# Transformer layer with segment memory, one core: another order of the first transposes and projections, nine more filler products, two-part masks without a wait between their parts, and a new order list

## The chip, the cores and the metric

The kernel runs on one NeuronCore of a Trainium2 chip. The metric is the time of one execution on the device, in microseconds (us). Engines: PE is TensorE (its weight loads are shown apart as PEld), DVE is VectorE, ACT is ScalarE, POOL is GpSimd, SP is SyncE, which here issues all DMA transfers.

## The reference

A pre-norm layer over 2048 tokens of width 640, in bf16: attention with 32 heads of 20, in four segments of 512 tokens, each with a causal softmax inside the segment and a linear memory of the segments before it; then an MLP of inner width 1728 with SiLU.

```python
phi = lambda t: jnp.where(t > 0, t + 1.0, jnp.exp(t))
for s in range(N):                                   # N = 4 segments of L = 512
    logits = jnp.einsum('bhqd,bhkd->bhqk', qs, ks) * scale + mask
    a_dot = jnp.einsum('bhqk,bhkd->bhqd', _softmax(logits, axis=-1), vs)
    num = jnp.einsum('bhld,bhde->bhle', phi(qs), M)
    den = jnp.einsum('bhld,bhd->bhl', phi(qs), z)[..., None] + 1e-06
    outs.append(g * (num / den) + (1.0 - g) * a_dot)
    M = M + jnp.einsum('bhld,bhle->bhde', phi(ks), vs)
    z = z + jnp.einsum('bhld->bhd', phi(ks))
...
h = x + _A_ref(_layernorm(x, axis=-1), A_wq, A_wk, A_wv, A_wo, A_beta)
h2 = h + _B_ref(_layernorm(h, axis=-1), B_w1, B_w2)  # silu(y @ w1) @ w2
```

## The kernel before

The four segments follow one another, overlapped: while the attention of one segment runs, the projections of the next and the MLP of the one before are put between. A segment is 4 blocks of 128 tokens.

Every step is a named task. In the order list a task stands as `name/engine:slots`; the suffix A, D or G puts a step on ACT, DVE or POOL, C runs a product as four 32-column products side by side, W makes one exponential of 2048 columns out of two of 1024, and the numbers are buffer slots (of PSUM banks, where PE is concerned). The list is the whole order: each engine runs its tasks in the order in which they stand there, and waits on semaphores for what it needs from others. A recorder (`Tracker`) works out these waits from what each instruction reads and writes.

The names that matter here, for block i of segment 0 and group g of 4 heads:

- `x0`, `x1`, `x2`: loads of block 0, block 1, and blocks 2 and 3 together. `w_q0`, `w_q1`, `w_k0`, `w_k1`: the query and key weights in two pieces each. `x4`, `x8`: later blocks.
- `fill`: products of zeros that nobody reads, at the start (L625).
- `n1_st`, `n1_rs`, `n1_ap`: statistics (DVE, for block 2 ACT), reciprocal root (POOL) and normalising (DVE) of a block; `n1_mn2` is the mean of block 2 on ACT. `n1_tp` transposes the block with five products against the identity (L816), and `n1_te` brings the result from PSUM into `tT` (ACT L825 or DVE L826).
- `pr000x`, `pr000y`, `pr001x`, `pr001y`: the first query and key projection, in halves of two token blocks (x is blocks 0 and 1, y is blocks 2 and 3), straight from the loaded weights as 32-column products (L740). Those that follow (`pr010` and on, L553 and L554) read weights that `re_` tasks have copied into another order (L733 and L735). `qe` brings a projection out of PSUM; `lsc0` is a small ACT step on the gate.
- `qk`, `e`, `mk`, `av`: scores (L991), exponential (ACT, L1012, or L1008 in one piece), causal mask (POOL, L1024) and weighted sum (L1047). The first exponential is `e0a2`. Score tiles a have one masked square, tiles b and e have two.
- `ex`, `pa`, `pb`: the three parts of phi. `kt` transposes phi of the keys by DMA into `phiKt` for the memory products; `vpad2` and `ve00` prepare the values of segment 0.
- `h1`, `th`, `s`, `h2`, `o`, `out`: the MLP and the output.

Where a task is several instructions of one engine, `run` records them: the first and the last carry the task's reads, the last its writes. For a task that reads and writes the same tile, such as a mask of two squares, the last instruction thus finds a read by the first and waits on POOL's own semaphore for it.

Of the kernel before, what the change touches and what calls it, by code (L numbers as in the profile page):

```python
# [6 lines left out]
ALU = mybir.AluOpType  # L7
# [37 lines left out]
class Tracker:  # L45
# [288 lines left out]
D = 640  # L334
# [36 lines left out]
x0:0 zpad:0 iota fill25:7 vpad0 x1:3 halfc mq0 x2:5,6 warm:0 w_q0:0 w_q1 n1_st0:5 w_k0:0 w_k1 w_wv:0 sel n1_st1:3  # L371
n1_rs0 epsc beta n1_ap0:1 fill5:5 n1_rs1 n1_st2:0,3 n1_st3:1 n1_tp0:0 n1_ap1:0 n1_mn2 n1_rs2 n1_te0:0 n1_rs3 n1_tp1:0
n1_ap2 re_wq1/G:0 n1_te1 n1_tp2:3 n1_ap3:2 x4:4,1,2,7 n1_te2/D x8:8,9,11,10 n1_tp3:6 re_wk0/G pr000x.0:2 n1_te3 re_wq3
pr000x.1 re_wq4/G pr001x.0:1 re_wk2/A qe000x/D:0 pr001y.0:5 re_wk1 pr000y.0:0 re_wq2/G re_wk3/A pr001y.1 pr001x.1
pr000y.1 qe001y qe001x/D eps0 pr010.0/C:2 qe000y re_wk4/G pa001:0 lsc0 ex001:0 qk0a0:4,0 pr010.1 vpad2 e0a2:3
pr011.0:7 re_wq0/G qe010/D:0 e0a0 pr011.1 lsc1 qk0b0:0,2 qe011/D pr020.0:6 e0b2:6 n1_st5:1 pr021.0:7 e0b0 qk0e0:4,2
n1_st6:2 pr020.1 e0e2:5 v00.0:0 pb001 n1_rs6 qe020/D:0 e0e0 v00.1 kt00:0 n1_st4:4 pr021.1 ve00:0 qk1a0:2,4 qe021/D
v02.0:6 e1a0:4 n1_rs4 v01.0:0 n1_st10:3 vt09:0 e1a2 n1_rs5 v01.1 vt06 pa011:1 mk0a ex021:2 qk1b0:4,2 ve01/D zf0 v02.1
mk1a e1b2:1 n1_ap4:2 mk0b v03.0:0 lsc2 ve02/D e1b0 n1_tr4:1 v03.1 lsc3 pa021:2 ex011:1 mk0e qk2a0:6,2 n1_ap5:0
pr040.0:4 e2a0:2 w_w1_1:0 ve03/D pr031.0:5 n1_tr5 e2a2 mq1 zf1 n1_st7:6 pr031.1 pr030.0:7 qe031:0 vt03 n1_st8:5  # L380
qk2b0:0,2 n1_rs7 ex031:0 pr030.1 vt00 e2b0:0 pr041.0:5 mq2 n1_ap6:1 qe030/D pr041.1 n1_rs8 n1_tr6 e2b2 pr040.1 pb011
qe041/D:0 mk1b av0:6 qe040 pa041:0 ex041:1 qk2e0:2,0 oe0/D:1 vt04 e2e0:3 n1_rs10 av1:5 n1_ap7:0 vt01 mk2b oe1/D:0
v10.0:4 e2e2 vt08 n1_st11:7 qk3a0:2,6 vt05 v10.1/C e3a2:1 mq3 mk2a vt07 ve10/D:0 e3a0 qk3b0:0,6 vt010 n1_st9:4
v11.0/C:4 e3b0:6 mk3a v11.1 mqr mk2e e3b2 vt02 qk4a0:0,2 ve11/D vt011 e4a2:4 td1:6 mk3b av2:7 nm1:1,1 n1_tr7 e4a0
oe2/D:0 qk4b0:3,5 vpad1 av3:2 e4b0:2 n1_ap10:3 n1_rs11 td2:7 e4b2 oe3/D:0 nm2:1 qk4e0:3,0 pr120.0:2 mk4b e4e0:5 pb041
pr120.1/C n1_ap8:2 e4e2 kt04:2 qk5a0:3,6 n1_rs9 pb021 pr100.0:5 qe120/D:0 e5a0:1 mm1 w_wo:0 pr100.1/C mk4e e5a2 w_w1_4
qe100/D:0 qk5b0:3,1 td3/C:0 n1_tr10:0 nm3:1 e5b2/W:3 v12.0:6 mzz mk4a n1_ap11:0 v12.1 kt01:1 mk5a pa100:0 td0/C:0 ve12
pa120:0 qk6a0:1,3 mk5b nm0:1 pr110.0/C:5 w_w1_3 e6a0:6 pa031:0 kt02:4 pr110.1 e6a2 qk6e0:1,6 qe110/D:0 av5:0 e6e2:0
pr111.0:5 e6e0 n1_tr8 pr111.1/C qk6b0:6,3 qe111/D av4:2 mk6e e6b0:3 n1_tr11 oe5/D:0 pr101.0/C:5 e6b2 pa110:0 qk7a0:0,6
oe4/D:1 w_w1_0 pr101.1 e7a2:1 mk6b n1_ap9:1 td4:2 pr130.0:3 e7a0 qe101/D n1_tr9 pr130.1 mk6a nm4:3 qk7b0:4,6 mk7a  # L390
e7b0:2 pb031 td5/C:2 v13.0/C:0 qe130/D:0 e7b2 kt03:3 v13.1/C nm5:2 av6:4 ex120:1 mk7b pa130:0 ex110:0 qk8a0:2,5 ve13/D
pr131.0:7 e8a0:4 mm0 pr131.1 oe6/D:0 e8a2 av7:0 qe131/D qk8b0:3,1 oe7/D:1 td6/C:7 e8b2:5 pr141.0:5 nm6:3 td7/C:0 e8b0
qk8e0:1,6 nm7:2 pr141.1/C e8e2:3 mk8b pr140.0:3 ot0:0 qe141/D:0 e8e0 pr140.1 pa101:0 qk9a0:6,4 mk8a qe140/D ot1 mz00:0
e9a0:6 mz02 mz03 mk8e pr121.0/C:1 pb110 mz04 e9a2 ot2 qk9b0:2,6 eps1 mz01 pr121.1/C e9b0:0 ma0:0 wo0.0:4 qe121/D e9b2
pb120 qk10a0:0,2 vt17:0 wo0.1 e10a0:2 mk9b vt19 wo1.0:6 rs0 e10a2 vt16 wo1.1 mk9a ot3 ex100:0 qk10b0:4,0 rs1 wo2.0:2
# [985 lines left out]
```

## Time and profile before

| | |
|---|---|
| median of 3 runs | 295.2 us (294.46 to 297.48) |
| the profiled execution | 296.44 us, span 294.7 us |
| PE busy | 280.0 us (95%) |
| ACT busy | 224.8 us (76%) |
| DVE busy | 212.6 us (72%) |
| POOL busy | 138.0 us (47%) |
| first product of the raw projection | 10.51 us |
| first exponential | 15.57 us |

The span runs from the first to the last instruction of the profiled execution; 1.74 us lie around it. A PE that is shown busy may be waiting inside a product's modelled length, so 95% doesn't mean that nothing is to be had there. The order listings below come from the built programs and hold no times.

### The profile page before, as it was taken

What the parts mean: (1) busy time and instruction counts of PE and PEld (TensorE: products, weight loads), DVE (VectorE), ACT (ScalarE), POOL (GpSimd) and SP (SyncE); (2) the same over time, 40 slices, a digit from 0 to 9 for tenths busy, and PEclk for the clock granted to TensorE, in tenths of its full rate; (3) what the DMA queues carried; (4) which work ended last, traced back from release to release, by engine and by line L of the source; (5) the groups of instructions that cost most, each with busy time, mean ns of one, the idle gap of its engine ahead of it and who ended that gap; (6) DMA issues with size and microseconds to landing.
All of it is one profiled execution on the core that took longest, in us unless ns stands there. A gap on an engine that the chain in (4) does not pass through costs nothing.

```text
span 294.7 us, 10305 instructions
## 1 busy us (share of the span) xinstructions
PE 280.0 (95%) x4460; PEld 155.8 (53%) x4482; DVE 212.6 (72%) x440; ACT 224.8 (76%) x290; POOL 138.0 (47%) x272
## 2 busy tenths in 40 slices
PE   7799879999999999999999999999899999999996
PEld 5545333445553445566653544656565457754674
DVE  5689988896998886959969882497386668526513
ACT  5699999999998999999689989999939940014400
POOL 4737877554840655827614572476063731200000
PEclk9799999999999999999999999999999999999999
DMA  6914518926552072144852244503110022350004
GB/s 209 361 52 79 107 38 208 228 44 96 130 110 64 21 219 52 24 88 77 93 126 76 48 82 65 87 3 65 33 24 2 2 45 47 66 137 1 2 4 158
DMA packets 48733, 24.84 MB, mean 84 GB/s; under 512 B 38896, under 2 KB 47472, under 8 KB 48688
## 3 DMA queue, kind: packets, MB, share of 16 engines
q1 hardware_dynamic: 48688, 24.19, 36.9%
q8 instruction: 35, 0.57, 0.8%
q14 instruction: 10, 0.08, 0.1%
HBM read 10.41 MB, written 2.62 MB: 44 GB/s over the span
## 4 chain that ended last, share of the span: by engine, by line
PE 70%; DVE 13%; ACT 7%; DMA 4%; POOL 2%; issue 2%; SPq 0%; DVEq 0%; ACTq 0%
PE ps_all L553 36%; PE ps_all L554 20%; PE ps_all L991 6%; ACT PT L1012 5%; PE ps_all L1047 4%; DVE xn_rot L807 2%; DVE stt L773 2%; DMA phiKt<-phiK 2%; DMA x_tok<-in_A_x_dram 1%; PE ps_all L740 1%; ACT PT L1008 1%; PE ps_all L1118 1%; POOL rst L801 1%; DVE oTs L1063 1%; DMA tT<-xn_rot 1%
## 5 line engine op out<-in xcount | busy, mean ns | idle before, releaser
L1012 ACT ACTIVATE PT<-ps_all 128x1024 bf16<-128x1024 f32 x134 | 129.7, 1030 | 11.4 <-PE ps_all L991 10.4
L1024 POOL TENSOR_SCALAR_AFFINE_SELECT PT<-PT 128x512 bf16<-128x512 bf16 x128 | 81.9, 652 | 68.9 <-ACT PT L1012 54.5
L1269 ACT ACTIVATE th<-ps_all 128x512 f32<-128x512 f32 (+1 forms) x56 | 31.3, 588 | 31.1 <-PE ps_all L553 25.9
L1275 DVE SCALAR_TENSOR_TENSOR sT<-th,ps_all 128x512 bf16<-128x512 f32 (+1 forms) x56 | 36.2, 662 | 16.3 <-ACT th L1269 16.2
L553 PE MATMUL ps_all<-tT,w_sb 128*128 128x512 bf16 x165 | 40.1, 379 | 1.0 <-issue 0.5
L553 PE MATMUL ps_all<-w_sb,sT 128*128 128x320 bf16 x270 | 39.9, 300 | 0.0
L553 PEld LDWEIGHTS ps_all<-w_sb,sT 128*128 128x128 bf16 x270 | 25.3, 98 | 12.0 <-issue 1.7
L773 DVE BATCH_NORM_STATS2 stt<-x_tok 128x6 f32<-128x320 bf16 x62 | 26.9, 476 | 2.2 <-DMA x_tok<-in_A_x_dram 2.1
L1312 DVE SCALAR_TENSOR_TENSOR x_tok<-ps_all,x_tok 128x640 bf16<-128x640 f32 (+1 forms) x17 | 13.2, 783 | 21.0 <-PE ps_all L554 15.2
L554 PE MATMUL ps_all<-w_sb,sT 128*32 128x320 bf16 x712 | 25.8, 299 | 0.0
L1008 ACT ACTIVATE PT<-ps_all 128x2048 bf16<-128x2048 f32 x13 | 24.5, 1883 | 1.2 <-PE ps_all L991 1.0
L553 PEld LDWEIGHTS ps_all<-tT,w_sb 128*128 128x128 bf16 x175 | 15.7, 98 | 18.3 <-issue 3.0
L1099 POOL TENSOR_TENSOR otok<-otok,om 128x320 bf16<-128x320 bf16 x24 | 18.2, 774 | 8.3 <-DVE otok L1086 4.5
L554 PE MATMUL ps_all<-tT,w_sb 128*32 128x512 bf16 x340 | 21.7, 380 | 0.2 <-DVE sT L1275 0.2
L554 PEld LDWEIGHTS ps_all<-w_sb,sT 128*32 128x32 bf16 x712 | 18.5, 97 | 5.7 <-issue 0.9
L799 POOL TENSOR_TENSOR rst<-mvt,eps_c 128x1 f32<-128x1 f32 x29 | 6.5, 226 | 31.5 <-DVE mvt L776 30.2
L553 PE MATMUL ps_all<-wv_sb,tT 128*128 128x320 bf16 x135 | 20.4, 300 | 0.3 <-ACT PT L1012 0.2
L807 DVE TENSOR_SCALAR xn_rot<-x_tok,mvt,rst 128x640 bf16<-128x640 bf16 x32 | 18.1, 572 | 1.9 <-POOL rst L801 1.2
L1234 DVE TENSOR_TENSOR x_tok<-ps_all,x_tok 128x640 bf16<-128x640 f32 x16 | 13.0, 810 | 7.1 <-PE ps_all L553 6.8
L801 POOL TENSOR_TENSOR rst<-rst,eps_c 128x1 f32<-128x1 f32 x29 | 16.6, 573 | 2.3
L1047 PE MATMUL ps_all<-PT,Vx 128*32 128x512 bf16 (+3 forms) x384 | 17.1, 300 | 0.3 <-ACT PT L1012 0.3
L1086 DVE TENSOR_TENSOR otok<-ps_all,rd 128x320 bf16<-128x320 f32 x32 | 15.7, 491 | 1.1
(117 smaller groups left out, 421.7 us busy)
## 6 DMA issues: line engine op xcount, KB each, us to landing
out_dram<-x_tok SPq DMA_DIRECT2D x15, 160.0 KB, 1.9
w_sb<-in_B_w_dram SPq DMA_DIRECT2D x5, 432.0 KB, 4.7
x_tok<-in_A_x_dram SPq DMA_DIRECT2D x3, 640.0 KB, 5.8
w_sb<-in_B_w_dram SPq DMA_DIRECT2D x3, 480.0 KB, 3.7
QKV<-QK SPq DMA_DIRECT2D x12, 72.0 KB
wv_sb<-in_A_wv_dram SPq DMA_DIRECT2D x1, 800.0 KB, 8.3
wo_sb<-in_A_wo_dram SPq DMA_DIRECT2D x1, 800.0 KB, 6.0
w_sb<-in_B_w_dram SPq DMA_DIRECT2D x1, 640.0 KB, 4.8
```

The costliest lines, as they stand in the source:

```text
L553: return [lambda e: e.matmul(out, lhsT=lhsT, rhs=rhs, start=start, stop=stop)]
L554: return [lambda e, p=p: e.matmul(out[p:p + 32, :], lhsT=lhsT[:, p:p + 32], rhs=rhs, start=start, stop=stop, tile_position=(0, p)) for p i ...
L773: T.add(DV, lambda e, hh=hh: e.bn_stats(out=stt[:, s, 6 * hh:6 * hh + 6], in_=xb[:, 320 * hh:320 * hh + 320]), reads=R((xa, xsub)), writes ...
L801: T.add(PO, lambda e: e.tensor_tensor(out=rst[:, s, :], in0=rst[:, s, :], in1=eps_c[:, 1:2], op=ALU.pow), reads=R((st, ["r"]), (C, ["half" ...
L807: T.add(eng, lambda e: e.tensor_scalar(out=xn_rot[:, xn.slot, :], in0=x_tok[:, b % 12, :], scalar1=mvt[:, s, 0:1], scalar2=rst[:, s, :], o ...
L1008: T.add(AC, lambda e: e.activation(out=o, in_=src, func=ACT.Exp, scale=SCALE), reads=[("ps", z.slot + q) for z in (a, b) for q in range(2) ...
L1012: T.add(AC, lambda e: e.activation(out=pt[:, pta.slot, q0:q0 + 2, 0:width], in_=sc3[:, b0:b0 + 2, 0:width], func=ACT.Exp, scale=SCALE), re ...
L1024: fns.append(lambda e, v=v: e.affine_select(out=v, in_=v, pattern=[[0, 4], [1, 128]], compare_op=ALU.is_ge, fill=0.0, base=0, channel_mult ...
L1047: fns.append(lambda e, j=j, r=r, h=h, pa=pa, pt=pt, co=co, q0=q0, ji=ji: e.matmul(bank(po)[32 * r:32 * r + 32, q0:hi], lhsT=vtile(vx)[:, j ...
L1099: T.add(PO, lambda e: e.tensor_tensor(out=o_dst, in0=o_dst, in1=m, op=ALU.add), reads=R((oma, WH), *osub), writes=R(*osub))
L1269: T.add(AC, lambda e: e.activation(out=th[:, tha.slot, lo:hi], in_=bank(ps)[:, lo:hi], func=ACT.Tanh, scale=0.5), reads=R((ps, [0])), writ ...
L1275: T.add(DV, lambda e: e.scalar_tensor_tensor(out=sT[:, f, lo:hi], in0=th[:, tha.slot, lo:hi], scalar=1.0, in1=bank(ps)[:, lo:hi], op0=ALU. ...
```

## The change

Three pieces of code and the list.

1. The four transposes of segment 0 write pairs of PSUM banks of their own: 2-3, 0-1, 6-7 and 4-5 for blocks 0, 1, 3 and 2. Before, blocks 0 and 1 shared the pair 0-1. Block 3 is now normalised and transposed before block 2, and the first three fifths of `pr000x` stand between the transposes of blocks 3 and 2.
2. The filler products are 25 + 4 + 8 + 2 in place of 25 + 5: 14 stand in place of the second five, so 39 in place of 30, nine more in all. The last two stand between two transposes.
3. A method `burst` takes the place of `run` in three tasks: masks, weight copies and the masked memory (`mb`). Its first instruction carries all waits, and the later ones none.
4. The whole list is new. Of the ten weight copies of segment 0, DVE makes none (two before), ACT three (two) and POOL seven (six). Nineteen exponentials are in one piece (13).

Below, PE's first rows before. `zpad` are filler products, `ident,xn_rot` transposes, `tT,sT` raw projection, `w2_sb` scores.

```order
L625 MATMUL ps_all<-zpad 128x256 x30
L816 MATMUL ps_all<-ident,xn_rot 128x128 x20
L740 MATMUL ps_all<-tT,sT 32x256 x80
L554 MATMUL ps_all<-tT,wqr 32x512 x12
L991 MATMUL ps_all<-w2_sb 128x512 x4
```

And in the changed kernel, whose lines are 12 further down:

```order
L637 MATMUL ps_all<-zpad 128x256 x37
L828 MATMUL ps_all<-ident,xn_rot 128x128 x10
L637 MATMUL ps_all<-zpad 128x256 x2
L828 MATMUL ps_all<-ident,xn_rot 128x128 x5
L752 MATMUL ps_all<-tT,sT 32x256 x12
L828 MATMUL ps_all<-ident,xn_rot 128x128 x5
L752 MATMUL ps_all<-tT,sT 32x256 x68
L566 MATMUL ps_all<-tT,wqr 32x512 x12
L1003 MATMUL ps_all<-w2_sb 128x512 x4
```

Twelve of the 80 raw products have moved ahead of the last transpose (block 2), and two filler products stand behind the second.

POOL at the same place before, with waits: `rst` are reciprocal roots (the two-step one is block 2's), `wqr` and `wkr` weight copies, `sT` is `vpad2`.

```order
L796 TENSOR_TENSOR rst<-mvt,eps_c 128x1 [waits s_dve]
L799 TENSOR_TENSOR rst<-mvt,eps_c 128x1 [waits s_pool,s_act]
L801 TENSOR_TENSOR rst<-rst,eps_c 128x1 [waits s_pool]
L796 TENSOR_TENSOR rst<-mvt,eps_c 128x1 [waits s_dve]
L735 COPY wqr<-sT 128x5x128 [waits l_w_q1,l_w_q0]
L735 COPY wkr<-sT 128x5x128 [waits l_w_k1,l_w_k0]
...
L640 MEMSET sT 128x4x32 [waits s_act,s_dve,s_pe,s_pool]
```

And in the changed kernel:

```order
L808 TENSOR_TENSOR rst<-mvt,eps_c 128x1 [waits s_dve]
L811 TENSOR_TENSOR rst<-mvt,eps_c 128x1 [waits s_act]
L813 TENSOR_TENSOR rst<-rst,eps_c 128x1 [waits s_pool]
L747 COPY wkr<-sT 128x5x128 [waits l_w_k1,l_w_k0]
...
L1036 AFFINE_SELECT PT<-PT 128x4x128 [waits s_act]
L747 COPY wkr<-sT 128x5x128
...
L652 MEMSET sT 128x4x32 [waits s_pool]
```

Block 3's root stands ahead of block 2's, POOL's first copy is one of the keys, and a mask of the first scores stands ahead of the last copies and `vpad2`.

DVE in the second segment's projections, where phi of the keys is written over a slot that a DMA transposition reads (`l_kt`), before:

```order
L925 TENSOR_SCALAR phiK<-w2_sb 128x512 [waits l_kt04]
L925 TENSOR_SCALAR phiK<-QK 128x512 [waits l_kt03]
```

And in the changed kernel:

```order
L937 TENSOR_SCALAR phiK<-w2_sb 128x512 [waits l_kt02]
L937 TENSOR_SCALAR phiK<-QK 128x512 [waits l_kt04]
```

The write no longer waits for `kt03`, which now stands behind it in the list; it waits for `kt04`. In the list that transposition stands 55 tasks ahead of the write; `kt03` stood 36 tasks ahead of it.

The diff, the list cut to its first lines:

```diff
+    def burst(self, eng, fns, reads=(), writes=()):
+
+        self.add(eng, fns[0], reads=reads, writes=writes)
+        for fn in fns[1:]:
+            seq = self.add(eng, fn).seq
+            for w in writes:
+                self._region(w).last_write = (eng, seq)
+            for r in reads:
+                st = self._region(r)
+                if r not in writes:
+                    st.reads[eng] = seq
...
-x0:0 zpad:0 iota fill25:7 vpad0 x1:3 halfc mq0 x2:5,6 warm:0 w_q0:0 w_q1 n1_st0:5 w_k0:0 w_k1 w_wv:0 sel n1_st1:3
-n1_rs0 epsc beta n1_ap0:1 fill5:5 n1_rs1 n1_st2:0,3 n1_st3:1 n1_tp0:0 n1_ap1:0 n1_mn2 n1_rs2 n1_te0:0 n1_rs3 n1_tp1:0
...
+n1_rs0 beta n1_ap0:0 n1_rs1 fill4:5 n1_st2:5,1 n1_st3:4 fill8:5 mq1 n1_tp0:2 n1_ap1:2 n1_rs3 n1_te0:1 n1_tp1:0 n1_rs2
+fill2:5 n1_ap3:3 n1_mn2 n1_te1 n1_tp3:6 n1_ap2 re_wq1/A:0 pr000x.0:3 n1_te3/D x4:2,10,11,1 n1_tp2:4 pr000x.1
...
-                T.run(eng, fns, R(*rr), R(*ww))
+                T.burst(eng, fns, R(*rr), R(*ww))
...
-                T.run(PO, fns, R((pta, subs)), R((pta, subs)))
+                T.burst(PO, fns, R((pta, subs)), R((pta, subs)))
...
-            T.run(PO, [lambda e: e.tensor_tensor(out=Mzb[:, mb.slot, 0:8:4, :], in0=Mz[:, 0:2, :], in1=MzM[:, 0:2, :], op=ALU.mult),
+            T.burst(PO, [lambda e: e.tensor_tensor(out=Mzb[:, mb.slot, 0:8:4, :], in0=Mz[:, 0:2, :], in1=MzM[:, 0:2, :], op=ALU.mult),
```

More of the change, by code (lines that the diff above doesn't have):

```diff
@@ L376 @@
[L376 to L395, printed above, removed]
@@ L466 @@
[L466 to L468 removed]
+x0:0 zpad:0 iota fill25:7 vpad0 x1:3 sel halfc mq0 x2:5,6 warm:0 w_q0:0 epsc w_q1 n1_st0:1 w_k0:0 w_k1 w_wv:0 n1_st1:0
+n1_rs0 beta n1_ap0:0 n1_rs1 fill4:5 n1_st2:5,1 n1_st3:4 fill8:5 mq1 n1_tp0:2 n1_ap1:2 n1_rs3 n1_te0:1 n1_tp1:0 n1_rs2
+fill2:5 n1_ap3:3 n1_mn2 n1_te1 n1_tp3:6 n1_ap2 re_wq1/A:0 pr000x.0:3 n1_te3/D x4:2,10,11,1 n1_tp2:4 pr000x.1
@@ new lines @@
+x8:9,8,4,7 n1_te2 pr001x.0:1 qe000x/D:0 re_wk1/G pr001x.1 re_wk2/A pr001y.0:2 re_wk4/G pr001y.1 qe001x pr000y.0:6
+qe001y pr000y.1 re_wk3/G pr010.0/C:0 pa001:2 qe000y ex001:1 re_wq2/G qk0a0:4,1 lsc0 pr010.1 e0a2:0 lsc1 pr011.0:7
+qe010/D:0 e0a0 pr011.1 qk0b0:0,2 qe011/D pr020.0/C:6 e0b2:3 mk0a pb001 pr020.1/C re_wk0/G n1_st4:3 e0b0 qk0e0:2,4
+pr021.0:7 re_wq4/G e0e0:5 n1_st5:1 v00.0:0 vpad2 n1_rs4 e0e2 v00.1 qe020/D:0 pr021.1 n1_rs5 n1_st10:7 ve00:0 qk1a0:2,4
+mk0b e1a0/W:4 qe021/D v02.0:6 v01.0:0 n1_st6:0 vt03:0 n1_rs10 v01.1 re_wq3/A qk1b0:2,4 vt00 ve01/D v02.1 e1b2/W:2
@@ new lines @@
+v22.0:6 mk10e vt111 n2_ap2:2 ve20 qk12a0:0,2 n2_ap0:1 v22.1 n2_tr2 e12a0/W:6 n2_rs3 pb101 v23.0:4 ve22/D mk11b v23.1
+mqr n2_ap3:0 ex140:0 qk12b0:0,2 n2_tr0 mk10b pr201.0/C:7 ve23/D e12b0:3 pr201.1/C pb130 n2_tr3 e12b2 td9/C:5 mm0
+av11:0 qe201/D:0 mm1 av10:6 nm9:2,0 ex131:1 eps0 kt10:0 td8/C:7 mzz oe11:1 qk12e0:3,1 eps1 oe10/D:0 pr211.0:5
+e12e2/W:2 mb0:1 pb131 pr211.1 pa111:0 kt13:2 eps2 h1_0_2_0.0:6 nm8:3 h1_0_2_0.1 pb140 ex111:2 qk13a0:1,3 w_w2_4
+th0_2_0:0 qe211/D:0 h1_0_1_0.0/C:7 e13a2:1 pb111 h1_0_1_0.1/C s0_2_0:0 pr221.0/C:0 w_w2_0 th0_1_0:1 pa121:1 ex121:0
@@ new lines @@
+rm10:5,3 s0_1_0 pr221.1/C e13a0 mn101:1,0 h1_0_0_0.0:7 qe221:0 h1_0_0_0.1/C mn100:0 qk13b0:3,0 th0_0_0:0
+h1_0_4_0.0/C:2 e13b0:0 w_w2_1 h1_0_4_0.1/C s0_0_0 kt11:4 th0_4_0:1 rm11:5,3 pr231.0/C:7 ex141:1 s0_4_0 e13b2 pr231.1/C
+mn111:2 h1_0_5_0.0/C:2 qe231:0 mk13b h1_0_5_0.1/C mn110:0 qk14a0:3,0 th0_5_0:0 pr200.0:7 mk12a e14a2:4 pr200.1 mk12e
+s0_5_0 h1_0_6_0.0:6 e14a0 td10:1 h1_0_6_0.1 mk13a qe200 nm10:2 qk14b0:4,2 th0_6_0:1 mk12b h1_0_8_0.0/C:0 e14b0:5
+s0_6_0 h1_0_8_0.1/C pa141:2 h1_0_3_0.0/C:1 e14b2 h1_0_3_0.1/C th0_8_0:0 av13:7 mk14b th0_3_0:1 s0_8_0 qk14e0:4,2
@@ new lines @@
+s3_4_0 h1_3_9_0.1 th3_2_0:0 h1_3_7_0.0/C:6 th3_9_0:1 s3_2_0 h1_3_11_0.1/C s3_9_0 h1_3_8_0.0/C:0 th3_11_0:0
+h1_3_7_0.1/C s3_11_0 h1_3_8_0.1/C th3_7_0:1 h1_3_12_0.0/C:7 th3_8_0:0 s3_7_0 h1_3_12_0.1/C s3_8_0 h1_3_13_0:1
+th3_12_0:1 h2_15_0/C:2 th3_13_0:0 s3_13_0 s3_12_0 h2_14_0/C:4 h2_14_1/C h2_15_1/C h2_12_0/C:0 h2_15_2/C h2_14_2/C
+h2_12_1/C h2_13_0/C:6 h2_15_3/C h2_14_3/C o15 h2_12_2/C o14 h2_12_3/C out14 out7 h2_13_1/C out11 o12 out15 h2_13_2/C
+h2_13_3_0/C out12 h2_13_3_1/C out9 o13_0 o13_1 out13_0 out13_1
```

151 lines of the change are left out of this document (75 added, 76 removed).

## The prediction

> **What bounds the kernel now.** I read the page, then the busy time by stage, the chain of waits, and the first 16 us one by one. From the page the granted clock in fortieths of the span, and the chain's shares:
>
> ```profile
> PEclk9799999999999999999999999999999999999999
> PE 70%; DVE 13%; ACT 7%; DMA 4%; POOL 2%; issue 2%; SPq 0%; DVEq 0%; ACTq 0%
> ```
>
> PE carries most of the chain, and the clock is short at one place only, near the start. By stage (length, then busy PE, PEld, DVE, ACT, POOL, then clock, DMA share, GB/s):
>
> ```profile
> 15.57:30.00 14.43, 14.16 (x108) 6.82 (x109) 12.81 (x32) 14.31 (x20) 7.46 (x20) 1.00 0.32 64
> 120.00:200.00 80.00, 79.27 (x1270) 43.87 (x1273) 61.56 (x131) 73.18 (x96) 43.91 (x76) 1.00 0.39 71
> ```
>
> From the first exponential at 15.57 us ACT is 99% busy (14.31 of 14.43), and from 120 to 200 us PE is (79.27 of 80). So what the first 15 us give should reach the end: ACT starts its stream earlier and PE follows. There the chain is:
>
> ```profile
> 6.03 0.84 ACT xn_rot L766 x2
> 6.89 0.93 ACT xn_rot L768 x2
> 8.67 0.64 POOL rst L796
> 9.40 0.68 DVE xn_rot L807
> 10.58 3.96 PE ps_all L740 x80
> ```
>
> Block 2's statistics, then block 3's root (L796, which stands behind block 2's on POOL), its normalising and, behind its transpose, the whole raw projection. The instructions around it:
>
> ```profile
> 8.63 0.44 PE L816 MATMUL ps_all<-ident,xn_rot 128*128 128x128 bf16 x5 [1.92 <-ACT tT L825]
> 7.28 0.15 DVE L779 TENSOR_SCALAR mvt<-mvt 128x1 f32<-128x1 f32 x1
> 7.35 0.44 DVE L807 TENSOR_SCALAR xn_rot<-x_tok,mvt,rst 128x640 bf16<-128x640 bf16 x1
> 7.81 0.68 ACT L825 ACTIVATE tT<-ps_all 128x640 bf16<-128x640 f32 x1
> 8.15 0.55 POOL L801 TENSOR_TENSOR rst<-rst,eps_c 128x1 f32<-128x1 f32 x1
> 9.99 0.81 DVE L826 CAST tT<-ps_all 128x640 bf16<-128x640 f32 x1
> 10.53 0.72 POOL L735 COPY wkr<-sT 128x640 bf16<-128x640 bf16 x1 [0.64 <-DMA sT<-in_A_wk_dram]
> 14.59 0.38 ACT L911 ACTIVATE w_sb<-ps_all 128x256 bf16<-128x256 f32 x1 [0.42 <-PE ps_all L740]
> 14.87 0.22 ACT L652 ACTIVATE bsel<-beta_bc 128x32 f32<-128x32 bf16 x1
> 14.99 0.62 ACT L918 ACTIVATE ex<-w_sb 128x512 bf16<-128x512 bf16 x1
> 15.57 1.94 ACT L1012 ACTIVATE PT<-ps_all 128x1024 bf16<-128x1024 f32 x2
> ```
>
> Block 1's transpose waited 1.92 us for its bank pair. The last key weights land at 10.5 us, a floor that the change doesn't move. Last the clock, first for all of PE, then for the transposes (L816) and the raw products (L740) alone:
>
> ```profile
> 4.14:7.55 3.41, 2.33 (x22) 1.00 0.95 316
> 7.55:10.97 3.42, 1.74 (x33) 1.00 1.06 375
> 10.97:14.38 3.41, 3.41 (x76) 0.50 1.06 347
> 7.55:10.97 3.42, 1.34 (x15) 1.00 1.06 375
> 7.55:10.97 3.42, 0.46 (x18) 1.00 1.06 375
> ```
>
> For 3.4 us PE ran at half clock, almost exactly the raw projection: 80 products, four side by side, so 20 steps in 3.96 us, 0.198 us each.
>
> **The change part by part.** *The start.* Block 3's root no longer waits behind block 2's two steps (its input is ready at 7.28 + 0.15 = 7.43): root 0.64 to 8.1, normalising 0.44 to 8.6, transpose 0.44 to 9.0. Block 2's root follows on POOL (0.2 + 0.55, 8.9), normalising to 9.4. With its own banks block 1 is transposed at 7.8, while ACT still copies block 0 (7.7 to 8.4); mean, then block 1's copy, to 9.3. The first raw products (`pr000x.0`) then start at 9.3 instead of 10.58, block 2's transpose goes between them at 9.7 to 10.1, and ACT copies it after one weight copy (about 0.7) at 10.1 to 10.8; block 3's copy on DVE (0.81) is done by 10.2. The second half (40 products, 10 steps) can thus start at 10.9, the first half being over by then, key weights (10.5) included.
>
> At full clock I estimate a step at 0.198 × 0.50 = 0.10 us, by the clock in the row above. So the second half ends at 11.9. ACT meanwhile makes a key weight copy (to 11.5) and three evacuations of 0.38, to 12.7; then the 0.62 of `ex` and the 0.22 of `lsc0`, which now stands behind it. First exponential at 13.5 instead of 15.57: **−2.1 us**. If the clock is halved over this stretch as before, the second half takes 2.0 us and ends at 12.9 to 13.9 (the first half is late too), ACT waits for it, and the first exponential comes at about 15.0: −0.6. So two thirds of this term hang on the clock.
>
> *The fillers.* Their end and their price, by half a microsecond of them:
>
> ```profile
> 5.63 0.38 PE L625 MATMUL ps_all<-zpad 128*128 128x256 bf16 x2
> 4.60:5.10 0.50, 0.50 (x7) 0.45 (x6) 1.00 0.90 305
> ```
>
> 0.07 to 0.1 us each. Seven of the nine end at 6.7 instead of 6.0, so block 0's transpose is over at 7.2 rather than 6.7, before ACT is free for it at 7.7; the two others fit between transposes that wait for DVE. Nothing on the path; without that cover 0.5. Do they hold the clock? In a 3.4 us stretch from 6.7 to 10.1 I count, by the rows above, four transposes (4 × 0.44), two fillers (0.2) and four steps (0.4): 2.4 of 3.4, 70%. Before, a stretch 68% busy (2.33 of 3.41) was followed by full clock and one 51% busy (1.74 of 3.42) by half. 70% is on the good side, narrowly.
>
> [...]
>
> *The weight copies.* DVE loses two, POOL makes seven. POOL's queue after the key weights land (10.5) by these rows (three-part copy, first half of `vpad2`):
>
> ```profile
> 12.85 1.03 POOL L735 COPY wkr<-sT 128x400 bf16<-128x400 bf16 x3
> 14.29 0.69 POOL L640 MEMSET sT<- 128x128 bf16 x1 [0.41 <-POOL wkr L735]
> ```
>
> Two copies of 0.72 and two of 1.03 bring it to 14.0; the mask now ahead waits for both first exponentials (13.5 + 1.94 = 15.4) and takes 0.63; two more copies and `vpad2` end near 19.0. ACT needs `vpad2` for `ve00` after six exponentials, at 19.6. Hidden, with 0.6 to spare.
>
> *The masks.* The group, and one pair as the chain has it:
>
> ```profile
> L1024 POOL TENSOR_SCALAR_AFFINE_SELECT PT<-PT 128x512 bf16<-128x512 bf16 x128 | 81.9, 652 | 68.9 <-ACT PT L1012 54.5
> 73.91 0.61 POOL PT L1024
> 74.52 0.06 issue
> 74.58 0.63 POOL PT L1024
> ```
>
> The wait that goes is 0.06 us; 128 masks make 32 tiles of one and 48 of two, so 48 × 0.06 = 2.9 us of POOL. POOL idles 68.9 us ahead of masks, and holds 2% of the chain: I take 0.1, between 0 and 2.9. `burst` changes nothing in the other two tasks, which read and write different tiles.
>
> *The transposition that DVE waited for:*
>
> ```profile
> 90.64 0.29 DVE L925 TENSOR_SCALAR phiK<-QK 128x512 bf16<-128x512 bf16 x1 [0.66 <-DMA phiKt<-phiK]
> 91.72 0.55 PE L1118 MATMUL ps_all<-Mzb,phiQ 32*128 32x168 bf16 x40 [0.39 <-DVE QK L912]
> ```
>
> The write now waits for an older transposition, so PE's 0.39 goes: −0.4, or 0 if that one is as late.
>
> *The rest of the list.* Pieces of exponentials, and products of 512 columns in whole and in four parts in the stretch 60 to 270 us:
>
> ```profile
> L1012 ACT ACTIVATE PT<-ps_all 128x1024 bf16<-128x1024 f32 x134 | 129.7, 1030 | 11.4 <-PE ps_all L991 10.4
> L1008 ACT ACTIVATE PT<-ps_all 128x2048 bf16<-128x2048 f32 x13 | 24.5, 1883 | 1.2 <-PE ps_all L991 1.0
> PEld ps_all L991 <- ACT PT L1008: 3.3, 10, 0.5
> L553 PE MATMUL ps_all<-tT,w_sb 128*128 128x512 bf16 x156 | 38.0, 379 | 0.9 <-issue 0.5 <-ACT QK L911 0.2
> L554 PE MATMUL ps_all<-tT,w_sb 128*32 128x512 bf16 x272 | 17.9, 380 | 0.2 <-DVE sT L1275 0.2
> ```
>
> Six more whole exponentials save ACT 6 × (2 × 1.03 − 1.88) = 1.1 us; one more weight copy (0.7) and evacuation (0.38) take it back: 0. The list has 10 more parts of the MLP's first product in four: some 25 units of 17.9/68 − 38.0/156 = 0.02, +0.5; I take +0.3, since some stand where ACT decides.
>
> Sum: −2.1 − 0.1 − 0.4 + 0.3 = −2.3. The profiled execution, 294.7 of span and 296.44 in all, would come to 294.1; it lies 1.2 above the median. From the median 295.2 I predict **292.9 us**.
>
> **The rivals.** *The clock falls all the same.* Then −0.6 in place of −2.1: 294.4. For: transposes alone didn't hold it, and 70% against 68% is thin. Against: the gap from 6.7 to 8.6 is filled now.
>
> *The masks count.* If PE's weighted sums wait for them, all 48 waits come off: another 2.8, 290.1. For: one such pair in the chain. Against: POOL's idle time.
>
> *Whole exponentials hold the banks (slower).* In one piece the banks come free 1.88 − 1.03 = 0.85 us later than the first half's, and PE's weight load waited 0.33 each time for it (3.3 in 10). Four of the new ones follow one another in segment 0, where ACT is the bound. If all six are exposed, 6 × (0.85 + 0.33) = 7.1: 300; it decides once PE has no other product ready for 0.85 us. Against: 13 of them cost 3.3 in all.
>
> **How the numbers follow.** Forecast 0.46, clock falls 0.22, masks count 0.20, whole exponentials 0.12. A measurement of this kernel can tell about 1%, 292.2 to 298.2, from no change. The forecast's own spread is 1 us or so, with two in five of it below 292.2: 0.18. Faster 0.18 + 0.20 = 0.38; same 0.28 + 0.22 = 0.50; slower 0.12. The range goes from the masks' 290.1 to 296.5: no gain at all, dearer products (+0.5), and 0.8 within the runs' spread; outside lie the slower rival and half a tenth on the low side.
>
> **What would show it.** Clock at 1.00 between 10 and 15 us and a first exponential at 13.5: the start is right. Half clock there and 15.0: the first rival. Idle time of PE after L1008 pieces (now at L1020): the third. If the first exponential is 2 us early and the end is not, the gain has been lost in the middle, and my claim that ACT's stream carries it is wrong. If `ve00` waits for POOL, the copies were too many.

## The result, and the profile after

The changed kernel takes 292.72 us (median of 8, 292.30 to 292.87) beside 295.76 us for the kernel before (8 executions, 294.24 to 297.48). The ratio is 0.9896, with a 95% interval of 0.9863 to 0.9929: about 1% faster. The profiled execution took 292.8 us, with a span of 291.1.

One thing must be known to read these times. In 17 of 80 executions of the kernel before, those timed beside the experiments, the granted clock averages 0.992 to 0.994 over the span, and they take 297.03 us on average; the other 63, at 0.998 to 1.000, take 295.29. The profiled execution of before, 296.44 us at 0.993, is of the rarer kind: it had half the clock for 3.41 us. The changed kernel lost its clock in none of its 8 (0.998 to 1.000). Where the text says "at full clock", it means the average over executions with 0.998 or more.

From the page of the changed kernel, the granted clock in fortieths of the span and the chain's shares:

```profile
PEclk9999999999999999999999999999999999999999
PE 79%; ACT 13%; DVE 4%; DMA 2%; POOL 1%; issue 1%; SPq 0%; DVEq 0%; ACTq 0%
```

DVE's share of the chain fell from 13% to 4%, and PE's and ACT's rose. Then PE's busy time and its clock in the first stretches (length, busy PE, clock, DMA share, GB/s), and all engines' (PE, PEld, DVE, ACT, POOL) from the first exponential on and in the middle:

```profile
4.14:7.55 3.41, 3.41 (x24) 1.00 1.01 315
7.55:10.97 3.42, 2.72 (x48) 1.00 1.05 375
10.97:14.38 3.41, 3.41 (x87) 1.00 1.02 329
13.86:28.29 14.43, 14.40 (x134) 6.92 (x136) 12.78 (x31) 14.41 (x19) 10.47 (x24) 1.00 0.40 94
120.00:200.00 80.00, 79.97 (x1270) 44.72 (x1270) 58.24 (x124) 73.70 (x97) 40.54 (x74) 1.00 0.41 73
```

ACT is busy as soon as the exponentials start, and PE in the middle, as before. Next the chain at the start:

```profile
6.65 0.90 DVE stt L785 x2
8.06 0.69 POOL rst L808
9.35 0.45 PE ps_all L828 x5
9.80 0.47 PE ps_all L752 x12
10.77 2.07 PE ps_all L752 x68
```

It is now block 3's statistics on DVE that set it, not block 2's on ACT, and the raw projection (L752) takes 0.47 and 2.07 us in place of 3.96. Blocks 2 and 3 landed at 6.65 us, 0.62 later than in the profile of before. Behind the raw projection, on ACT and on POOL:

```profile
13.86 5.72 ACT L1024 ACTIVATE PT<-ps_all 128x1024 bf16<-128x1024 f32 x6
19.59 0.71 ACT L880 ACTIVATE sT<-ps_all 128x640 bf16<-128x640 f32 x1
18.48 0.46 POOL L653 MEMSET sT<- 128x48 bf16 x1
```

The first exponential starts at 13.86 us (before: 15.57), `ve00` (L880) starts at 19.59 without a wait, and `vpad2` has ended on POOL at 18.94. Last the groups that stand beside those of before: exponentials in two parts and in one, masks, and PE's waits for the long ones.

```profile
L1024 ACT ACTIVATE PT<-ps_all 128x1024 bf16<-128x1024 f32 x122 | 117.9, 1030 | 7.9 <-PE ps_all L1003 6.8
L1020 ACT ACTIVATE PT<-ps_all 128x2048 bf16<-128x2048 f32 x19 | 35.7, 1878 | 3.5 <-PE ps_all L1003 3.4
L1036 POOL TENSOR_SCALAR_AFFINE_SELECT PT<-PT 128x512 bf16<-128x512 bf16 x128 | 81.6, 666 | 71.6 <-ACT PT L1024 59.5
PEld ps_all L1003 <- ACT PT L1020: 5.4, 15, 0.6
```

### The profile page after: what moved, and what is told of

It reads as the page before. It is cut to its first block, busy times and chain, and to the rows that moved or that the text cites. A ratio compares the mean times of both kernels' runs of the same rounds, so it can differ in the third digit from the quotient of the medians.

```text
span 291.1 us, 10526 instructions
## 1 busy us (share of the span) xinstructions
PE 283.0 (97%) x4587; PEld 156.9 (54%) x4587; DVE 208.7 (72%) x435; ACT 224.7 (77%) x286; POOL 138.1 (47%) x275
## 4 chain that ended last, share of the span: by engine, by line
PE 79%; ACT 13%; DVE 4%; DMA 2%; POOL 1%; issue 1%; SPq 0%; DVEq 0%; ACTq 0%
PE ps_all L565 41%; PE ps_all L566 23%; ACT PT L1024 9%; PE ps_all L1003 7%; PE ps_all L1059 5%; ACT PT L1020 2%; DMA x_tok<-in_A_x_dram 2%; PE ps_all L1130 1%; PE ps_all L752 1%; PE ps_all L1268 1%; ACT ex L930 1%; POOL PT L1036 1%; DVE om L1149 1%; ACT oTs L1073 1%; PE ps_all L1189 1%
## 5 line engine op out<-in xcount | busy, mean ns | idle before, releaser
L1024 ACT ACTIVATE PT<-ps_all 128x1024 bf16<-128x1024 f32 x122 | 117.9, 1030 | 7.9 <-PE ps_all L1003 6.8
L1020 ACT ACTIVATE PT<-ps_all 128x2048 bf16<-128x2048 f32 x19 | 35.7, 1878 | 3.5 <-PE ps_all L1003 3.4
L565 PE MATMUL ps_all<-w_sb,sT 128*128 128x320 bf16 x252 | 37.0, 299 | 0.0
L565 PE MATMUL ps_all<-tT,w_sb 128*128 128x512 bf16 x151 | 36.4, 380 | 0.0
L565 PEld LDWEIGHTS ps_all<-w_sb,sT 128*128 128x128 bf16 x252 | 23.7, 98 | 11.0 <-issue 1.7
L566 PE MATMUL ps_all<-w_sb,sT 128*32 128x320 bf16 x784 | 28.8, 299 | 0.0
L566 PE MATMUL ps_all<-tT,w_sb 128*32 128x512 bf16 x436 | 27.1, 380 | 0.0
L566 PEld LDWEIGHTS ps_all<-w_sb,sT 128*32 128x32 bf16 x784 | 20.1, 97 | 6.7 <-issue 0.9
L565 PEld LDWEIGHTS ps_all<-tT,w_sb 128*128 128x128 bf16 x151 | 13.6, 98 | 16.1 <-issue 1.9
L819 DVE TENSOR_SCALAR xn_rot<-x_tok,mvt,rst 128x640 bf16<-128x640 bf16 x32 | 16.7, 533 | 2.5 <-POOL rst L813 1.3
L1059 PE MATMUL ps_all<-PT,Vx 128*32 128x512 bf16 (+3 forms) x384 | 16.9, 300 | 0.2 <-ACT PT L1024 0.2
```

The costliest lines, as they stand in the source:

```text
L565: return [lambda e: e.matmul(out, lhsT=lhsT, rhs=rhs, start=start, stop=stop)]
L566: return [lambda e, p=p: e.matmul(out[p:p + 32, :], lhsT=lhsT[:, p:p + 32], rhs=rhs, start=start, stop=stop, tile_position=(0, p)) for p i ...
L819: T.add(eng, lambda e: e.tensor_scalar(out=xn_rot[:, xn.slot, :], in0=x_tok[:, b % 12, :], scalar1=mvt[:, s, 0:1], scalar2=rst[:, s, :], o ...
L1020: T.add(AC, lambda e: e.activation(out=o, in_=src, func=ACT.Exp, scale=SCALE), reads=[("ps", z.slot + q) for z in (a, b) for q in range(2) ...
L1024: T.add(AC, lambda e: e.activation(out=pt[:, pta.slot, q0:q0 + 2, 0:width], in_=sc3[:, b0:b0 + 2, 0:width], func=ACT.Exp, scale=SCALE), re ...
L1059: fns.append(lambda e, j=j, r=r, h=h, pa=pa, pt=pt, co=co, q0=q0, ji=ji: e.matmul(bank(po)[32 * r:32 * r + 32, q0:hi], lhsT=vtile(vx)[:, j ...
```

## The experiments

All were timed beside the kernel before. The column "at full clock" is the average over the executions that kept it, with its standard error, and the difference is to the 295.29 us (± 0.07) of the kernel before.

| kernel | executions, of them clock lost | median | at full clock | difference |
|---|---|---|---|---|
| before | 80, 17 | 295.49 | 295.29 ± 0.07 | |
| changed | 8, 0 | 292.72 | 292.64 ± 0.08 | −2.65 |
| before, 22 fillers in place of 5 | 12, 0 | 296.56 | 296.56 ± 0.15 | +1.27 |
| changed, 30 fillers | 6, 0 | 292.74 | 292.84 ± 0.14 | −2.45 |
| changed, a wait per product | 6, 0 | 293.32 | 293.31 ± 0.10 | −1.98 |
| before, burst | 12, 3 | 294.90 | 294.50 ± 0.20 | −0.79 |
| new start alone | 13, 0 | 294.57 | 294.64 ± 0.15 | −0.65 |
| burst and new rest of the list | 12, 2 | 294.14 | 293.99 ± 0.13 | −1.30 |
| before, other slots of phiK | 12, 2 | 295.46 | 295.30 ± 0.21 | 0.0 |
| changed, four exponentials split | 6, 0 | 292.85 | 292.84 ± 0.28 | −2.45 |
| changed up to `qk10a0`, old list behind | 12, 0 | 297.46 | 297.53 ± 0.19 | +2.24 |
| new start, other slots of phiK | 12, 0 | 294.41 | 294.48 ± 0.11 | −0.81 |
| changed, burst in eight ticks only | 6, 0 | 292.82 | 292.87 ± 0.13 | −2.42 |
| before, `td24` in bank 3 | 12, 2 | 295.81 | 295.65 ± 0.25 | +0.36 |

**The clock by fillers.** The old list with 22 fillers in two places, where it had five, to hold the clock and change nothing else:

```diff
-... n1_ap0:1 fill5:5 n1_rs1 n1_st2:0,3 n1_st3:1 n1_tp0:0 n1_ap1:0 ...
+... n1_ap0:1 fill12:5 n1_rs1 n1_st2:0,3 n1_st3:1 n1_tp0:0 fill10:5 n1_ap1:0 ...
```

> The kernel before with more filler products alone: 12 in place of the second 5, and 10 between the first two transposes, where PE waited 1.92 us. Clock theory (the half-clock stretch from 11 to 14.4 us is what the change removes): the clock stays at 1.00, the raw projection takes 2.1 us in place of 3.96, the first exponential comes at 13.8 in place of 15.57, and the time is 1.7 us below the kernel before, with executions that lie within 1 us of each other. Rival (the order of transposes and the list bring the gain, the clock little): within 0.5 us of the kernel before.

The clock held in all 12 executions, and the time is 296.56 us, ratio 1.0034 (1.0017 to 1.0052) to the kernel before: slower. In its profile the first exponential starts at 14.00 us, 1.6 earlier than in the profile of before, and the lead lasts to 85 us; the span ends at the same 294.7. The start itself is no worse for the fillers: 8.05 us from the landing of blocks 2 and 3 to the first exponential, as in the old start at full clock (7.95 to 8.01). The lead is lost behind it, 1.1 us of it between 85 and 93 and 0.5 between 117 and 123. So a start that is early does not by itself reach the end. Why all twelve executions are slower than the old start at full clock, by 1.27 us on average, one profile doesn't show.

**The nine fillers.** The changed kernel with 25 and 5 fillers, everything else as it is:

```diff
-... n1_rs1 fill4:5 n1_st2:5,1 n1_st3:4 fill8:5 mq1 n1_tp0:2 ... n1_rs2 fill2:5 n1_ap3:3 ...
+... n1_rs1 fill5:5 n1_st2:5,1 n1_st3:4 mq1 n1_tp0:2 ... n1_rs2 n1_ap3:3 ...
```

> The changed kernel with 30 filler products, 25 and 5 in one stretch, in place of 39. Clock theory: the stretch without products from 6 to 8 us is back, so the clock falls in some executions; those take about 1.5 us more (294.2), others 292.7, and the spread grows to over 1 us. Rival (the denser transposes and the projection between them are enough): 292.7 in all executions, clock at 1.00.

292.74 us, ratio 0.9903 (0.9878 to 0.9929), and the clock held in all six: the nine cost nothing that can be measured, and without them nothing was lost here. Six executions can't rule out a rare loss: were it as frequent as in the kernel before, one in five, six without one would still come in about a quarter of the cases.

**The burst, taken away and alone.** The changed kernel with `run` in all three tasks, and the kernel before with `burst` in all three:

```diff
-                T.burst(PO, fns, R((pta, subs)), R((pta, subs)))
+                T.run(PO, fns, R((pta, subs)), R((pta, subs)))
```

> The changed kernel with the waits between the parts of masks, weight copies and the masked memory as before. Forecast: 0.1 us more (292.8), since POOL idles ahead of masks. Rival (masks count): up to 2.9 us more, 295.6.

> The kernel before with only the waits between parts of one task taken away (masks, weight copies, masked memory). Forecast: 0.1 us less than the kernel before. Rival (masks count): up to 2.9 us less.

293.32 us, ratio 0.9920 (0.9892 to 0.9947), without the burst; 294.90 us, ratio 0.9974 (0.9945 to 1.0003), with it alone. At full clock that is 0.67 us on the new list and 0.79 (± 0.2) on the old one. From the chain of the changed kernel without the burst, at the pair of masks that PE's weighted sum (L1059) waits for:

```profile
35.70 0.60 POOL PT L1036
36.29 0.06 issue
36.35 0.64 POOL PT L1036
37.00 0.04 issue
37.04 0.76 PE ps_all L1059 x16
```

The wait of 0.06 us between the two masks is there, on the chain. In the changed kernel the same pair, in one burst, takes 1.19 us in place of 1.30 (35.70 to 37.00):

```profile
36.00 1.19 POOL PT L1036 x2
```

Elsewhere the gain is seen only in sum: by the exponentials made, the kernel without the burst is 0.3 us behind the one of the next experiment from the first exponential on (its blocks 2 and 3 landed 0.24 us later), still 0.3 at 36 us, and 0.7 at 60. So some 0.4 us build up between, in these two profiles.

**Burst in the first eight ticks.** The changed kernel, with `run` for all other masks, the weight copies and the masked memory. The expectation says that these ticks go up to about 95 us; by the exponentials made up to then they end at about 56 us.

```diff
-                T.burst(PO, fns, R((pta, subs)), R((pta, subs)))
+                (T.burst if int(name[:-1]) < 8 else T.run)(PO, fns, R((pta, subs)), R((pta, subs)))
```

> The changed kernel with the burst only for the masks of its first eight ticks (up to about 95 us); the masks behind them, the weight copies and the masked sums (L1212) wait per product, as before the change. With the burst everywhere it is 292.7 us, nowhere 293.3. Theory from the profiles: the exponentials of the kernel without bursts fall behind between 39 and 67 us and nowhere else, so the first eight ticks carry the gain: 292.6 to 292.9 us. Rival: the masks cost a little at many places, or at the end: 293.0 to 293.4 us.

292.82 us, ratio 0.9911 (0.9878 to 0.9944). At full clock that is 0.44 us (± 0.16) of the 0.67 that the burst is worth on this list, and 0.23 (± 0.15) short of the changed kernel. So the masks of the first eight ticks bring most of it, and within the errors all.

**The start alone and the rest alone.** The first has the kernel before's code (a wait per product) and the changed list up to `pr011.1`, the second the changed kernel's code and the old list up to there. Five and one buffer slots behind the joint had to be renumbered, and in the first `re_wq3` stands on ACT ahead of `qk1b0`.

```diff
-n1_rs0 epsc beta n1_ap0:1 fill5:5 n1_rs1 n1_st2:0,3 n1_st3:1 n1_tp0:0 n1_ap1:0 n1_mn2 n1_rs2 n1_te0:0 n1_rs3 n1_tp1:0
+n1_rs0 beta n1_ap0:0 n1_rs1 fill4:5 n1_st2:5,1 n1_st3:4 fill8:5 mq1 n1_tp0:2 n1_ap1:2 n1_rs3 n1_te0:1 n1_tp1:0 n1_rs2
...
 pr011.1
```

> The kernel before with the changed list up to `pr011.1` (transposes in banks of their own, block 3 ahead of block 2, a projection between, the copies of the key and query weights moved), and its own list behind that; the masks as before, a wait per product. Fillers: 25 + 4 + 8 + 2, as in the changed list. Theory of the prediction: the start is the whole gain, it reaches the end, and what follows is worth nothing, so 293.0 to 293.6 us. Rival, formed after the first four experiments: at full clock the start gains only 0.6 to 0.7 us (first exponential at about x2's landing + 7.3 instead of + 8.0), and the kernel's old list gives some of that back at the transpositions between 77 and 91 us, so 294.7 to 295.4 us against 295.4 before. What tells them apart besides the time: under the rival the first exponential is early by 0.5 us or more and the exponentials behind 91 us are not.

> The changed kernel with the old list up to `pr011.1` (30 fillers, two banks for the transposes, block 2 ahead of block 3) and its own list behind that; masks as one burst. Theory of the prediction: masks 0.1, a wait on kt03 0.4, other products +0.3, so 295.0 to 295.4 us. Rival: the masks are worth 0.5 and the rest of the list about 1.4, so 293.2 to 293.8 us with a first exponential at x2's landing + 7.9.

294.57 us, ratio 0.9960 (0.9936 to 0.9984), for the start, and 294.14 us, ratio 0.9948 (0.9924 to 0.9973), for the rest with the burst. At full clock the start is worth 0.65 us and the rest 1.30, of which the burst has about 0.7. Together they make 1.95; the change as a whole gives 2.65. So 0.7 us (± 0.2) come only when both are there. Whether the two parts help each other, or the joint in each of the mixed lists costs something, these runs don't tell apart.

The profiled execution of the first is its slowest of 13 (296.18 us, the others 293.84 to 294.93), so what it shows at 85 us need not be in the others. Its chain there:

```profile
84.96 0.15 DVE otok L1085
85.11 4.86 DMA phiKt<-phiK
89.97 0.02 issue
89.99 0.30 DVE phiK L924
90.32 0.70 DVE QK L911
91.07 0.55 PE ps_all L1117 x40
```

To compare the profiles along their length I took, for each, the time by which it had made the same number of exponential columns (163,840 in all), and show how many us earlier that was than in the profile of before, at whose times the columns stand:

| kernel | 23.8 | 67.4 | 85.5 | 92.6 | 101.0 | 199.6 | 209.3 | span |
|---|---|---|---|---|---|---|---|---|
| new start alone | 2.0 | 2.0 | 2.0 | 0.8 | 0.6 | 0.6 | 0.6 | 0.2 |
| new start, other slots | 1.5 | 1.5 | 1.5 | 1.4 | 1.9 | 1.9 | 1.9 | 1.4 |
| changed to `qk10a0`, old behind | 2.5 | 3.3 | 2.4 | 1.3 | 1.1 | −0.3 | −0.3 | −0.3 |
| burst and new rest | −0.3 | −0.5 | −0.6 | −0.2 | 0.3 | 0.3 | 1.0 | 0.6 |
| changed | 1.6 | 2.4 | 2.4 | 2.8 | 3.2 | 3.2 | 4.0 | 3.6 |

The two kernels with the new list throughout gain 0.9 us between 85.5 and 101 and 0.8 between 199.6 and 209.3; the others go from a loss of 1.4 to a gain of 0.3 at the first place, and gain nothing at the second. These are single executions; the kernel with burst and new rest had lost its clock.

**The wait for kt03.** The old list, and then the new start with the old list behind, with slots 0 and 1 of phiK changed over from `pa101` on (seven numbers), so that phi isn't written where kt03 still reads:

```diff
-pa101:0 ... pa131:1 ... pa111:0 ... pa141:0 ... pa201:0 ... pa241:1 ... pa211:1
+pa101:1 ... pa131:0 ... pa111:1 ... pa141:1 ... pa201:1 ... pa241:0 ... pa211:0
```

> The kernel before with seven numbers changed: from `pa101` on, slots 0 and 1 of phiK change places, so that the phi write of block pair 1's first key column takes a slot whose reader (kt01) was issued long before, and does not wait for kt03's transposition, which SP issues 25 us into a stretch of transposes and copies without a gap. Nothing else moves. Theory of the prediction: this wait alone is worth 0.4 us, so 295.0 us. Rival 1: it is where the lead is lost, and most of what the rest of the list gives comes from it: 294.2 to 294.7 us. Rival 2: it only takes the last place in the chain from the transposes of SP, which are as late: 295.3 to 295.5 us, no change.

> The kernel of the run with the new start and the old list behind it (294.6 us), with slots 0 and 1 of phiK changed over from `pa101` on, so that the phi write of block pair 1 no longer waits for kt03. Nothing else. In that kernel's profile a lead of 2.0 us on the profile before fell to 0.8 us between 85 and 93 us, in the chain at `DMA phiKt<-phiK`. Theory: this wait eats a lead that SP's queue cannot follow, and the lead now reaches the end: 293.8 to 294.2 us. Rival: the transposes `DMA tT<-xn_rot` before it hold the chain as long, and nothing changes: 294.4 to 294.8 us.

295.46 us, ratio 1.0002 (0.9975 to 1.0030): nothing. On the new start 294.41 us, ratio 0.9960 (0.9938 to 0.9982): 0.16 us (± 0.19) from the same kernel without the edit, where 0.6 was expected. The wait is gone from that profile's chain, and PE is at its products in its place:

```profile
85.93 1.89 PE ps_all L552 x8
87.82 0.33 PE ps_all L990 x4
88.15 0.98 PE ps_all L553 x16
89.88 0.48 PE ps_all L1117 x40
```

So most executions seem not to pay for this wait, or to lose as much elsewhere without it. In another profile of the old list at full clock (that with `td24` in bank 3, below) kt03 is in the chain too, issued at 84.4, and the lead falls by 0.1 there; it falls by 1.1 to 1.3 in the three profiles in which SP, behind its other transposes and copies, came to issue it at 84.7 or later though the kernel was 1.6 to 2.4 us ahead (22 fillers, start alone, changed up to `qk10a0`).

**Whole exponentials.** The four added whole exponentials of the first 45 us in two halves each:

```diff
-... e1a0/W:4 ... e1b2/W:2 ... e2a2/W:6 ... e2b2/W:1
+... e1a0:4 e1a2 ... e1b2:2 e1b0 ... e2a2:6 e2a0 ... e2b2:1 e2b0
```

> The changed kernel with the four added whole exponentials of its first 45 us (e1a0, e1b2, e2a2, e2b2: one instruction of 1024 columns over two banks) as two halves each, as the kernel before has them; banks and order unchanged. Theory of the prediction: whole or split costs nothing: 292.5 to 293.0 us. Rival (whole exponentials hold two banks so long that PE waits): faster than the changed kernel, 291.8 to 292.4 us. Rival on the other side (one instruction in the place of two spares ACT a fixed cost in a stage that ACT sets): slower, 293.1 to 293.6 us.

292.85 us, ratio 0.9904 (0.9868 to 0.9941): no difference.

**The late part of the list.** The changed kernel, with its own list up to `qk10a0` and the old one behind. The expectation puts `qk10a0` at about 100 us; it stands at about 66. So the place at 85 to 101 us has the old order as well.

> The changed kernel with its own list only up to about 100 us (up to `qk10a0`) and the old list behind that. The changed kernel is at 292.7 us, the kernel before at full clock at 295.3. Theory formed from the profiles so far: the old list loses 0.7 us a second time near 204 us, where `nm24` must free the bank of `td24` for `qk28b0` and stands on DVE behind three other instructions; so 293.3 to 293.5 us. Rival (theory of the prediction: what stands behind the start is worth nothing): 292.6 to 292.9 us. Rival on the other side: the late part holds all that the list is worth, 294.0 us or more.

297.46 us, ratio 1.0063 (1.0038 to 1.0088). At full clock that is 4.9 us behind the changed kernel and 2.2 behind the kernel before. It is on the side of the last expectation, whose reason doesn't give it: the late part can't hold more than the whole list is worth. In its profile 1.1 us of the lead go between 85.5 and 92.6, where its chain has `DMA phiKt<-phiK` for 4.79 us, 1.5 us between 117 and 123, and nothing is gained at 204. In the second of these stretches, chain and waits:

```profile
116.91 0.32 PE ps_all L1002 x6
117.23 1.20 issue
118.44 0.28 PE ps_all L1002 x2
PE ps_all L1002 <- issue: 1.2, 1, 1.2
```

In the middle of eight score products PE stood for 1.2 us, for nothing that the profile shows. The chain of the kernel with 22 fillers has 0.36 us of this at 118.7 us, that of the changed kernel none between 108 and 121. What it is stays open. What the run shows is that the front of one list and the back of another don't add up. That each was laid out for the arrival times of its own front is the likely reason, and isn't shown.

**A bank at 204 us.** In the profile of before the chain runs through DVE there (residual add, normalising, a phi product, then the two steps of `nm24`), and PE waits:

```profile
203.78 0.82 DVE x_tok L1312
204.61 0.75 DVE xn_rot L807
205.35 0.77 DVE phiQ L931
206.12 0.18 DVE rd L1084
206.32 0.50 DVE otok L1086
206.96 0.42 PE ps_all L991 x8
```

In the changed kernel no DVE work is in the chain at that place:

```profile
201.19 0.36 PE ps_all L1003 x4
201.54 0.02 issue
201.56 1.94 ACT PT L1024 x2
203.50 1.77 ACT PT L1020
```

The old list, with `td24` in another bank:

```diff
-... qk28a0:6,4 pb330 td24:2 e28a2:6 ...
+... qk28a0:6,4 pb330 td24:3 e28a2:6 ...
```

> The kernel before with one number changed: `td24` (the transposition of a tick's output) writes bank 3 in the place of bank 2, so that `qk28b0`, which takes bank 2, does not wait for `nm24` (L1084, L1086) behind the residual add, a normalisation and a phi product on DVE (203.8 to 206.8 us of the chain of the kernel before). 295.3 us before at full clock. Theory: this bank is the late place of the list, worth 0.7 us: 294.4 to 294.8 us. Rival: PE then waits for ACT's exponentials or for the next bank, and nothing is gained: 295.2 to 295.5 us.

295.81 us, ratio 1.0011 (0.9988 to 1.0033): nothing. But the edit didn't do what it was meant to: `qk28b0:4,2` takes the pair of banks 2 and 3, and in its trace PE waits for the same DVE instruction (the bracket is the idle time ahead):

```profile
206.05 0.40 PE L991 MATMUL ps_all<-QK 20*128 20x384 bf16 x8 [0.62 <-DVE otok L1086]
```

So this bank has not been tested. That the new list has no such wait, and gains 0.8 us at that place in two profiles, is seen; that the one is the cause of the other is only argued.

No kernel of these is better than the changed one: the three that come within 0.25 us of it differ from it by less than twice their error.

## Why the prediction was right or wrong

The time was right, and the sign. The sum of which it was made was not: at full clock the 2.65 us are about 0.65 from the start, 0.7 from the masks, 0.6 from the rest of the list, and 0.7 that the start and the rest give only together. The clock adds 1.74 us in one execution of before in five, 0.37 on average.

**The start, −2.1.** In the profiles the mechanism is right: full clock between 10 and 15 us, and the first exponential 7.2 us behind the landing of blocks 2 and 3 in place of 9.5, at 13.86 with a landing 0.6 later. The profiles of four old starts that kept their clock have 7.95 to 8.05 us and those of eight new starts 7.2 to 7.8, so about 0.5 is the order's and 1.5 the clock's (9.5 less 8.0): "two thirds of this term hang on the clock" was right as well. A step of the raw projection at full clock, estimated at 0.10 us, measured 0.12 (2.07 us for 17). What failed is the step "From the median 295.2 I predict": the sum was made on an execution with a lost clock and taken from a median of executions that mostly kept it. By the prediction's own terms, 0.7 of the 2.1 could be had there, and the sum would have been 294.3. The other terms made up for it; that 292.9 lies within 0.2 us of the measured time is luck.

**What the first 15 us give should reach the end.** Not by itself. The 22 fillers brought 1.6 us on the profile of before, and nothing reached the end; the start alone brings its 0.65. At 85 to 93 us a lead can be lost on the old list.

**The fillers, 0,** and the half-filled stretch, 70%: the stretch from 6.10 to 9.51 us was 81% busy (2.75 of 3.41). Without the nine it is 71%, and held too. The rival in which the clock falls all the same did not come.

**The weight copies.** `vpad2` ends at 18.94 and is needed at 19.59; forecast were 19.0 and 19.6.

**The masks, −0.1, between 0 and 2.9.** Mis-sized: 0.67 to 0.79 us, most of it, within the errors all, from the first eight ticks. POOL's idle time of 69 us was read over the whole span, but the masks that bind are those of the first fifth of it, where POOL is busy for 10.47 of 14.43 us and, as the chain at 36 us shows, a weighted sum waits for the second of a pair. The rival's 2.8 did not come either.

**The transposition that DVE waited for, −0.4 or 0:** 0 on the old list, 0.16 ± 0.19 on the new start. In the profiles of the old list it is in the chain and costs next to nothing or over 1 us, as SP's queue stands.

**The rest of the list, +0.3.** Wrong in sign: about −0.6, and −1.3 behind the new start. I counted its products and pieces, that is, its work; its worth seems to lie in when they come, which a count doesn't show. Which step of the order brings it stays open: the two that were tried alone, the wait for kt03 and the bank at 204 us, gave nothing, and the second edit didn't take the wait away. DVE's share of the chain, 13% before and 4% after, is at most a hint.

**Whole exponentials, 0.** Right: four of the six split again, nothing changes that can be measured (0.2 ± 0.3). PE's weight loads do wait for them for 5.4 us in 15 (3.3 in 10 before), at no cost that the split could show.

## What to carry to other kernels

Before subtracting a stall that a profile shows, ask whether the median has it: the granted clock of each timed execution told here that the profiled one was of the rarer kind (17 of 80). An engine's idle time over the span is no cover for the one instruction that another engine waits for: POOL idled 69 us ahead of masks here, and the waits between them cost 0.67 to 0.79. And a new order's worth can't be summed from the work that it moves: time the front and the back of the list each alone on the chip, and don't count on their adding up: here they gave 0.65 and 1.30 us alone, and 2.65 together.

## What the runs showed of the hardware

In the profile of before the granted clock first rose at 4.11 us of the span, fell to 0.50 after 6.83 us, rose again 3.41 after that and fell 279.89 later, 0.5 ahead of the end. In that of the changed kernel it rose at 6.1 us and fell 286.72 later, behind the end of the span. These lengths are 2, 1, 82 and 84 times 3.413 us. With burst and the new rest the stretch at half clock, 10.31 to 13.72 us, is 3.41 long as well. So for each profile I laid stretches of 3.41 us end to end over its start, in the two that lost the clock so that one of them is the stretch at half clock. PE's busy time in the least busy of them (length, busy, clock), with the stretch behind it, for the profile of before, for burst with the new rest, and for burst on the old list:

```profile
7.50:10.92 3.42, 1.69 (x31) 1.00 1.06 375
10.92:14.33 3.41, 3.41 (x72) 0.50 1.06 347
```

```profile
6.90:10.31 3.41, 1.65 (x19) 1.00 1.02 354
10.31:13.72 3.41, 3.11 (x53) 0.50 1.04 344
```

```profile
6.58:9.99 3.41, 1.68 (x21) 1.00 1.03 351
9.99:13.40 3.41, 3.06 (x96) 1.00 1.03 332
```

The clock was lost behind 1.69 and 1.65 us and kept behind 1.68; it was kept behind 1.76 and 1.86 in two more profiles of the old start. So at this share, about half, the clock went either way, and the old start lies there: of 128 executions with it and its 30 fillers 26 lost the clock. Nor is a less busy stretch always followed by a loss: in the two profiles with 1.76 and 1.86 one laid elsewhere, from 7.55 to 10.97 us, has 1.26 and 1.45 us of products, and the clock was 1.00 behind it. For the changed kernel and for the same with 30 fillers:

```profile
6.10:9.51 3.41, 2.75 (x30) 1.00 1.02 328
```

```profile
5.95:9.36 3.41, 2.43 (x36) 1.00 1.01 346
```

They are well above 1.69, as are the other profiles of the new start (2.75 to 3.06); none of its 69 executions here lost the clock.

Of the busy time of the three stretches of the old start, 1.34 us (before), 1.33 (burst, new rest) and 1.21 (burst) are transposes, and 0.35, 0.32 and 0.47 are PE's other products; of the two of the new start, 1.05 and 1.35 are transposes and 1.70 and 1.08 others. What decides whether the clock holds, five stretches don't show.
